# Another order of the first stage of an attention and SwiGLU kernel

## The chip, the cores and the metric

The kernel runs on one core of a Trainium2 chip. The metric is device time in microseconds (us) of one execution. The engines are TensorE (PE: matmuls; PEld is its weight load), VectorE (DVE), ScalarE (ACT), GpSimd (POOL) and SyncE (SP); each works through its own queue in order, and the engines wait for each other on semaphores. POOL, SP and ACT also issue DMA transfers.

## What is computed

Attention over 4 batches, 8 heads, 768 tokens and 64 channels, in which a query sees the 96 last keys and the 8 first (global) ones, with a bias that falls with distance; then a SwiGLU block on the 3072 tokens.

```
scores = scale * q @ k.T + bias        # bias = -slope[h] * dist, -1e9 outside the window
a      = softmax(scores)
x      = (a @ v) as 3072 x 512
g      = x @ w_gate                    # 512 x 1536
out    = (g * sigmoid(g) * (x @ w_val)) @ w_out
```

## The kernel before

The program is one string, ORDER, of steps such as `c.0.1.0`; a table, WORK, gives the function of each, and a loop calls them one after the other. So ORDER sets the order of the instructions in every engine's queue. An engine doesn't pass a waiting instruction. PSUM banks are handed out in the order of the string too: score and value products take turns on two double banks (`double`), all else takes the longest-freed of four single banks (`single`, `release`).

Work goes batch by batch. In a batch the heads are taken as four pairs (hp 0 to 3); keys are cut into seven chunks of 120, each with the 8 global keys in front; a batch's queries are two halves. For batch 0, a pair's scores are four units: u 0 and 1 for the first half, 2 and 3 for the second. Two groups g of two pairs make up the 512 channels of x. The block then runs on half batches t, with 12 column groups f of 128.

The steps that the text names, with their arguments and engine:

- `Lf`, `Lh.i.half.h0.h1`, `Lr.b.i.h`: rows of k (i = 0) or q (i = 1); `Lv.b.c`: rows of v of a chunk; `Lw.which.n.g`: gate (0) or value (1) weights of the columns 512 n on, upper or lower half of the rows; `LG`: global rows of v into vG; `L4`: rows of batch 1. All but Lf are issued by POOL.
- `fill.n` (L344): n warm products of 256 columns, whose results nobody reads.
- `cast` and `T.hp.half.i` (L363, TensorE transposes), `k.hp.half.e` (L371) and `q.hp.half.e` (L395), the copies out of PSUM by engine e; `U`, `kw`, `qw` are the same for pairs of batch 1; `D` is a transposing DMA and `K` spreads its keys.
- `sl.h` (L331, DVE): slope of a head times the identity; `B.hp.u` (L457, PE): writes the bias into a score bank; `c.b.hp.u` (L467, PE): adds the scores; `x.b.hp.u` (L481, ACT): the exponential.
- `M.h.part` (L336, ACT): mask of a head, 216 columns for part 0 and 432 for part 1; `m.b.hp.u.e` (L490): multiplies exponentials by the masks of the pair's two heads on engine e (P is POOL, V is VectorE). Units with a `B` need no mask.
- `G.b.c0.c1.e` (L274): copies the global rows of v from vG into the chunks c0 to c1 - 1 of vS, on e.
- `w.b.g.half.what` (L524, PE): denominators (what = 0, den) and values (1 and 2, num); `i`, `r` (DVE): inverts and spreads the denominators; `p.b.g.half.e` (L573): writes x.
- `g.t.f` and `v.t.f` (L582, PE): gate and value products, four matmuls each over the rows of the weights; `ga`, `gb` are the first and last two of a gate product; `t` (ACT, tanh), `s` and `h` (DVE); `o`, `e`: product with w_out and its copy to HBM.

The value products of batch 0's first half (`w.0.0.0.1`) read chunks 0 to 2 of vS; those of the second half (`w.0.0.1.1`) read chunks 2 to 6. `m.0.0.2.P` reads part 1 of the masks of heads 0 and 1, `m.0.3.1.P` that of heads 6 and 7.

Of the kernel before, what the change touches and what calls it, by code (L numbers as in the profile page):

```python
# [49 lines left out]
g.0.4 g.0.7 L4.1.0 t.0.4 h.0.0 s.0.4 t.0.7 s.0.7 g.0.6 t.0.6 L4.0.0 M.4.1 s.0.6 ga.0.2 gb.0.2 t.0.2  # L50
M.3.1 v.0.4 Lv.0.5 h.0.4 v.0.6 c.0.2.3 s.0.2 m.0.0.2.P c.0.2.2 x.0.2.3 h.0.6 x.0.2.2 w.0.0.1.0
i.0.0.1 r.0.0.1 g.0.5 t.0.5 G.0.4.7.P s.0.5 v.0.2 v.0.7 M.2.1 h.0.7 g.0.8 h.0.2 g.0.9 M.5.1 t.0.8
s.0.8 v.0.5 Lv.0.3 M.6.0 g.0.11 Lv.0.4 t.0.9 s.0.9 h.0.5 Lv.0.6 Lw.1.2.0 t.0.11 s.0.11 g.0.10 t.0.10
c.0.3.3 s.0.10 m.0.2.3.V m.0.2.2.P U.1.0 x.0.3.3 m.0.3.3.V U.0.1 U.1.1 kw.1.A U.0.0 qw.1.A w.0.0.1.1
w.0.0.1.2 p.0.0.1.V w.0.1.1.1 w.0.1.1.0 Lw.1.2.1 Lr.1.0.6 w.0.1.1.2 i.0.1.1 c.1.1.1 Lr.1.0.7 v.0.9
r.0.1.1 p.0.1.1.V kw.0.A Lr.1.1.7 qw.0.A v.0.8 x.1.1.1 h.0.8 h.0.9 M.7.0 v.0.10 Lr.1.0.4 g.1.6
Lr.1.1.4 c.1.0.0 t.1.6 x.1.0.0 c.1.0.1 D.1.3.0 v.0.11 h.0.11 h.0.10 g.1.0 t.1.0 s.1.0 x.1.0.1
c.1.1.0 g.1.9 t.1.9 g.1.7 s.1.6 t.1.7 s.1.9 g.1.1 s.1.7 x.1.1.0 g.1.3 v.1.0 t.1.3 Lr.1.0.5 h.1.0
v.1.6 D.1.2.0 c.1.0.2 s.1.3 h.1.6 c.1.1.2 K.1.3.A t.1.1 K.1.2.V g.1.5 s.1.1 x.1.1.2 M.2.0 M.0.0
v.1.9 h.1.9 v.1.7 t.1.5 h.1.7 Lr.1.1.6 Lr.1.1.5 D.1.3.1 s.1.5 g.1.2 t.1.2 x.1.0.2 s.1.2 D.1.2.1  # L60
v.1.5 g.1.11 t.1.11 h.1.5 m.1.0.1.P Lo.1 s.1.11 Lr.3.0.5 g.1.4 Lo.0 m.1.1.2.P v.1.3 h.1.3 t.1.4
m.1.0.2.V Lo.2 g.1.8 t.1.8 v.1.1 h.1.1 s.1.4 c.1.2.1 x.1.2.1 c.1.3.1 s.1.8 v.1.8 v.1.11 h.1.11 v.1.2
Lr.2.0.3 x.1.3.1 h.1.2 Lv.1.1 c.1.2.2 x.1.2.2 c.1.3.0 v.1.4 Lr.2.0.0 h.1.4 o.0.1.0 Z.1.V m.1.1.0.P
M.4.0 Lr.2.0.2 m.1.3.1.V G.1.0.7.S g.1.10 Lv.1.2 o.0.1.1 o.0.1.2 x.1.3.0 c.1.2.0 x.1.2.0 h.1.8
c.1.3.2 x.1.3.2 o.0.1.3 e.0.1 Lr.2.1.1 M.1.0 v.1.10 o.0.0.0 o.0.0.1 Lv.1.0 m.1.2.1.V m.1.1.1.V
Lr.2.0.1 t.1.10 m.1.3.0.V o.0.0.2 o.0.0.3 o.0.2.0 o.0.2.1 m.1.2.2.V Z.2.V Lv.1.3 s.1.10 m.1.0.0.V
w.1.0.1.0 e.0.0 w.1.0.0.1 w.1.0.0.0 h.1.10 m.1.2.0.P w.1.1.0.0 Lv.1.5 w.1.1.0.1 D.2.1.0 w.1.1.0.2
w.1.0.0.2 i.1.0.0 i.1.1.0 Lr.2.1.0 o.0.3.0 o.0.3.1 Lr.3.1.2 r.1.0.0 p.1.0.0.D D.2.0.0 o.0.3.2
o.0.3.3 Lv.1.6 r.1.1.0 Lv.1.4 Lr.2.1.4 p.1.1.0.D o.0.2.2 e.0.3 o.0.2.3 e.0.2 g.2.1 i.1.0.1 r.1.0.1
t.2.1 s.2.1 Lr.2.1.3 Lr.2.1.7 g.2.7 t.2.7 s.2.7 g.2.3 t.2.3 v.2.7 h.2.7 g.2.0 v.2.3 K.2.1.V Lr.3.0.1  # L70
g.2.5 s.2.3 K.2.0.V t.2.0 w.1.0.1.1 m.1.3.2.P w.1.1.1.1 w.1.1.1.0 D.2.0.1 s.2.0 w.1.1.1.2 Lr.2.1.2
D.2.1.1 i.1.1.1 w.1.0.1.2 o.0.4.0 t.2.5 s.2.5 Lr.2.0.7 Lr.2.0.6 o.0.4.1 o.0.4.2 o.0.4.3 p.1.0.1.D
v.2.0 h.2.3 e.0.4 Lr.3.1.4 h.2.0 n.1.1.1 g.2.4 t.2.4 r.1.1.1 p.1.1.1.P D.2.3.0 v.2.1 h.2.1 s.2.4
g.2.11 t.2.11 s.2.11 g.2.2 t.2.2 Lr.2.0.4 v.2.4 h.2.4 g.2.6 t.2.6 Lr.2.0.5 s.2.2 s.2.6 v.2.5 g.3.5
t.3.5 c.2.1.1 Lr.2.1.5 x.2.1.1 c.2.0.0 x.2.0.0 h.2.5 v.2.6 s.3.5 D.2.2.0 g.3.4 g.2.10 t.2.10
Lr.2.1.6 c.2.0.1 Lv.3.5 c.2.1.0 x.2.1.0 K.2.3.V h.2.6 v.2.11 s.2.10 h.2.11 Lr.3.0.3 v.2.2 o.0.5.0
g.3.3 x.2.0.1 h.2.2 t.3.4 g.2.8 t.2.8 Lr.3.0.0 m.2.0.0.V m.2.0.1.P o.0.5.1 o.0.5.2 s.2.8 s.3.4
o.0.5.3 D.2.3.1 e.0.5 Lr.3.1.6 v.2.10 h.2.10 v.3.5 t.3.3 g.3.10 t.3.10 D.3.0.0 c.2.0.2 h.3.5 s.3.10
g.3.6 t.3.6 Lr.3.1.3 g.2.9 x.2.0.2 s.3.3 v.2.8 h.2.8 t.2.9 v.3.10 D.2.2.1 G.2.0.7.S c.2.3.0 h.3.10
x.2.3.0 s.3.6 c.2.3.2 x.2.3.2 m.2.1.1.P K.2.2.A o.1.0.0 v.3.4 o.1.0.1 o.1.0.2 m.2.1.0.P v.2.9  # L80
m.2.3.2.V s.2.9 h.2.9 w.2.0.0.0 i.2.0.0 h.3.4 c.2.2.1 c.2.2.0 g.3.9 r.2.0.0 x.2.2.0 Lr.3.0.7 g.3.7
x.2.2.1 t.3.9 s.3.9 o.1.0.3 e.1.0 Lv.2.0 c.2.1.2 x.2.1.2 c.2.3.1 v.3.9 h.3.9 v.3.6 h.3.6 D.3.1.1
t.3.7 Lv.2.1 x.2.3.1 g.3.11 t.3.11 Lr.3.0.2 v.3.7 Lv.2.2 g.3.8 m.2.3.0.P t.3.8 m.2.2.0.P s.3.7 h.3.7
m.2.3.1.V v.3.3 h.3.3 s.3.8 w.2.0.0.1 w.2.0.0.2 m.2.2.1.P w.2.1.0.0 i.2.1.0 r.2.1.0 Lv.3.4 Lr.3.0.4
w.2.1.0.1 w.2.1.0.2 Lr.3.1.0 D.3.1.0 s.3.11 g.3.1 t.3.1 K.3.1.A g.3.2 t.3.2 s.3.1 s.3.2 o.1.1.0
o.1.1.1 p.2.1.0.D Lr.3.1.7 o.1.1.2 o.1.1.3 g.3.0 v.3.11 e.1.1 t.3.0 p.2.0.0.D s.3.0 v.3.1 g.4.9
Lv.2.3 c.3.1.0 x.3.1.0 t.4.9 h.3.11 h.3.1 c.3.1.1 v.3.2 h.3.2 v.3.8 h.3.8 g.4.5 Lr.3.1.1 x.3.1.1
t.4.5 s.4.5 g.4.6 t.4.6 Z.3.V D.3.0.1 Lv.2.4 c.3.1.2 x.3.1.2 c.2.2.2 x.2.2.2 s.4.6 v.4.9 v.4.5 s.4.9
h.4.9 h.4.5 v.3.0 h.3.0 g.4.8 K.3.0.A t.4.8 v.4.6 s.4.8 v.4.8 m.2.1.2.P Lv.2.6 o.1.2.0 o.1.2.1
m.2.2.2.V D.3.3.1 o.1.2.2 h.4.6 Lv.3.2 g.4.2 t.4.2 h.4.8 m.3.1.2.V D.3.2.0 c.3.0.0 x.3.0.0 w.2.1.1.0  # L90
Lv.2.5 K.3.2.A m.2.0.2.P w.2.0.1.0 i.2.0.1 i.2.1.1 w.2.1.1.1 w.2.1.1.2 w.2.0.1.1 w.2.0.1.2 r.2.1.1
o.1.5.0 r.2.0.1 Lr.3.1.5 D.3.2.1 g.4.11 o.1.5.1 o.1.5.2 Lv.3.6 o.1.2.3 p.2.1.1.D o.1.5.3 p.2.0.1.D
Lr.3.0.6 c.3.2.2 e.1.2 e.1.5 s.4.2 c.3.2.1 g.4.1 t.4.1 g.5.7 s.4.1 o.1.4.0 o.1.4.1 o.1.4.2 t.5.7
s.5.7 t.4.11 x.3.2.2 m.3.1.0.P s.4.11 v.5.7 o.1.4.3 h.5.7 v.4.2 e.1.4 g.5.6 h.4.2 t.5.6 g.4.0 v.4.1
x.3.2.1 o.1.3.0 m.3.2.1.P t.4.0 s.5.6 o.1.3.1 s.4.0 h.4.1 D.3.3.0 g.4.4 t.4.4 s.4.4 g.4.7 c.3.0.2
x.3.0.2 Lv.3.1 c.3.0.1 o.1.3.2 o.1.3.3 x.3.0.1 e.1.3 v.4.11 K.3.3.V c.3.2.0 c.3.3.2 h.4.11 x.3.3.2
m.3.3.2.P t.4.7 v.5.6 h.5.6 v.4.4 Lv.3.3 h.4.4 g.5.8 x.3.2.0 v.4.0 v.5.8 m.3.2.0.P s.4.7 t.5.8 s.5.8
# [591 lines left out]
```

## Time and profile before

| | |
|---|---|
| Time, median of 3 runs | 241.35 us (241.26 to 241.36) |
| Profiled execution | 241.18 us |
| Its span, first to last instruction | 239.4 us |
| TensorE busy | 232.8 us, 97% of the span |
| VectorE, ScalarE, POOL busy | 159.0, 117.5, 128.4 us |
| TensorE busy from 0 to 6 / 6 to 9 / 9 to 12 / 12 to 15 us | 4.80 / 2.93 / 2.24 / 2.29 |
| TensorE busy from 15 to 19 / 24 to 37 / 60 to 220 us | 4.00 / 13.00 / 159.75 |
| TensorE, warm products (26) | until 7.6 to 8.1 us in four groups |
| DMA read from HBM | 28.52 MB |

Times in the profile's rows are from the start of the span. A row of the timeline has start, length, engine, line, operation, output and input tiles and the number of instructions merged in it; in brackets stands how long its engine sat idle before it and what ended that. In the row of 40 slices, a digit is a tenth of busy time. In the chain of waits a row is start, length and what ran. A DMA row has the tensor, the issuing queue, the number of transfers, their size and the time from issue to landing.

### The profile page before, as it was taken

The numbers are of one execution on the slowest core, as the hardware profiler recorded it, in microseconds if no ns is written. First come the engines' busy times: TensorE is split into PE (matmuls) and PEld (weight loads), VectorE is DVE, ScalarE is ACT, GpSimd is POOL, SyncE is SP. The second block draws the span as 40 slices with busy tenths as digits, with TensorE's granted clock in tenths as the row PEclk, the third lists the DMA queues.
The fourth block names the chain that finished last, engine by engine and source line by source line (L and its number), as shares of the span: only waits on it lengthen the run. The fifth ranks groups of instructions, "written<-read, shape, count | busy, mean of one in ns | idle before, by whom it ended". The sixth has DMA issues, their size and how long they took to land.

```text
span 239.4 us, 5661 instructions
## 1 busy us (share of the span) xinstructions
PE 232.8 (97%) x2284; PEld 133.5 (56%) x2284; DVE 159.0 (66%) x351; ACT 117.5 (49%) x225; POOL 128.4 (54%) x136
## 2 busy tenths in 40 slices
PE   8889999999999999999999999999999999999994
PEld 5555666555455655546555555556566555565452
DVE  4697888787769676677876844687878843577000
ACT  3878777876405355666474446652142323232121
POOL 8996887599899098999974004799100000000000
PEclk9999999999999999999999999999999999999999
DMA  7999999999999999997999025413020110200042
GB/s 174 179 191 205 204 171 155 149 153 179 161 139 147 170 147 123 176 100 126 126 151 107 3 88 93 72 11 23 0 90 3 44 42 10 83 1 0 0 178 88
DMA packets 88714, 25.50 MB, mean 107 GB/s; under 512 B 78536, under 2 KB 85744, under 8 KB 88688
## 3 DMA queue, kind: packets, MB, share of 16 engines
q0 software_dynamic: 67520, 13.81, 69.9%
q1 hardware_dynamic: 20624, 10.94, 21.7%
q10 hardware_dynamic: 544, 0.39, 0.6%
q8 instruction: 18, 0.29, 0.5%
q14 instruction: 8, 0.07, 0.1%
HBM read 28.52 MB, written 6.29 MB: 145 GB/s over the span
## 4 chain that ended last, share of the span: by engine, by line
PE 94%; DVE 3%; ACT 2%; issue 0%; ACTq 0%
PE gps L588 27%; PE vps L588 26%; PE ops L623 25%; PE sc L475 5%; PE num L538 4%; PE den L538 2%; PE warm L346 2%; PE trs L367 1%; ACT at L485 1%; PE sc L462 1%; DVE at L503 1%; PE trs L405 1%; DVE slopeI L332 1%; DVE qT L396 0%; DVE xT L575 0%; ACT osb L633 0%
## 5 line engine op out<-in xcount | busy, mean ns | idle before, releaser
L588 PE MATMUL gps<-xT,wg 128*128 128x408 f16 (+1 forms) x384 | 72.9, 326 | 0.0
L595 ACT ACTIVATE th<-gps 128x360 f32<-128x360 f32 (+1 forms) x96 | 46.5, 492 | 52.9 <-PE gps L588 47.8
L588 PE MATMUL vps<-xT,wv 128*128 128x408 f16 (+1 forms) x384 | 72.5, 326 | 0.0
L610 DVE TENSOR_TENSOR hT<-vps,sl 128x360 f16<-128x360 f32 (+3 forms) x108 | 52.8, 509 | 23.6 <-PE vps L588 22.1
L600 DVE SCALAR_TENSOR_TENSOR sl<-th,gps 128x360 f32<-128x360 f32 (+1 forms) x96 | 51.5, 548 | 23.9 <-ACT th L595 22.5
L623 PE MATMUL ops<-wo,hT 128*128 128x512 f16 (+1 forms) x300 | 67.0, 371 | 0.0
L503 POOL TENSOR_TENSOR at<-at,masks 128x432 f16<-128x432 f16 (+3 forms) x36 | 47.8, 1347 | 28.9 <-ACT at L485 27.7
L588 PEld LDWEIGHTS <-wv 128*128 128x128 f16 x384 | 36.7, 98 | 26.8 <-issue 1.4
L588 PEld LDWEIGHTS <-wg 128*128 128x128 f16 x384 | 36.7, 98 | 25.6 <-issue 0.7
L485 ACT ACTIVATE at<-sc 128x864 f16<-128x864 f32 (+2 forms) x52 | 42.3, 841 | 13.0 <-PE sc L475 12.8
L623 PEld LDWEIGHTS <-hT 128*128 128x128 f16 x300 | 28.8, 98 | 30.0 <-issue 0.2
L633 ACT ACTIVATE osb<-ops 128x512 f32<-128x512 f32 (+1 forms) x25 | 14.3, 580 | 48.9 <-PE ops L623 45.5
L265 POOL DMA_DIRECT2D vS<-in_v_dram x28 | 25.6, 919 | 1.6 <-DVE vS L283 1.4
L306 POOL DMA_DIRECT2D qst<-in_q_dram x20 | 17.1, 869 | 0.0
L306 POOL DMA_DIRECT2D kst<-in_k_dram x20 | 17.1, 858 | 0.0
L575 DVE TENSOR_TENSOR xT<-num,rb 128x720 f16<-128x720 f32 (+1 forms) x15 | 14.1, 948 | 1.5 <-PE num L538 1.0
L475 PE MATMUL sc<-qT,kT 64*128 64x216 f16 (+4 forms) x232 | 14.7, 240 | 0.3
L475 PEld LDWEIGHTS <-kT 64*128 64x128 f16 x232 | 8.1, 94 | 9.6 <-issue 7.7
L555 DVE STREAM_TRANSPOSE dT<-den 128x384 f32<-128x384 f32 (+1 forms) x16 | 9.5, 595 | 4.7 <-PE den L538 4.4
L503 DVE TENSOR_TENSOR at<-at,masks 128x864 f16<-128x864 f16 (+2 forms) x21 | 10.5, 537 | 1.9 <-ACT at L485 1.9
L538 PE MATMUL num<-at,vS 128*32 128x216 f16 (+4 forms) x512 | 11.6, 233 | 0.0
L538 PEld LDWEIGHTS <-vS 128*32 128x32 f16 x512 | 9.1, 96 | 1.3 <-issue 1.1
(58 smaller groups left out, 117.1 us busy)
## 6 DMA issues: line engine op xcount, KB each, us to landing
out_dram<-osb SPq DMA_DIRECT2D x23, 256.0 KB, 2.1
vS<-in_v_dram POOLq DMA_DIRECT2D x24, 120.0 KB, 5.7
kst<-in_k_dram POOLq DMA_DIRECT2D x20, 96.0 KB, 5.2
qst<-in_q_dram POOLq DMA_DIRECT2D x20, 96.0 KB, 5.2
wg<-in_moe_w_gate_dram POOLq DMA_DIRECT2D x6, 256.0 KB, 8.5
wv<-in_moe_w_val_dram POOLq DMA_DIRECT2D x6, 256.0 KB, 7.9
wo<-in_moe_w_out_dram POOLq DMA_DIRECT2D x3, 512.0 KB, 8.4
k<-in_k_dram POOLq DMA_DIRECT2D x3, 192.0 KB, 5.9
```

Source lines behind the costliest of these rows:

```text
L265: nc.gpsimd.dma_start(out=v_of(b)[NG:NG + n, c, :, :], in_=v[b, :, KC * c:KC * c + n, :].rearrange("h p d -> p h d"))
L306: nc.gpsimd.dma_start(out=rows_of(i, b, h // 2)[:, :, h % 2, :], in_=KQ[i][b, h].rearrange("(t p) d -> p t d", p=128))
L475: nc.tensor.matmul(sc[:, hi, col:col + n], lhsT=kTs[hp][r, 128 * c:128 * c + 128], rhs=qTs[b, hp][r, q0:q0 + n], start=fresh, stop=True, s ...
L485: nc.scalar.activation(out=at[:, :, 0:w], in_=scs.pop((b, hp, u))[:, :, 0:w], func=AF.Exp, scale=scale)
L503: ENG[e].tensor_mul(a2, a2, m[:, :, m0:m0 + n])
L538: nc.tensor.matmul(dst[r, o:o + n], lhsT=vSs[b][:, c, 4 * g + j, what - 1::2] if what else ones[:, 0:32], rhs=ats[b, hp, u][:, j % 2, col: ...
L588: nc.tensor.matmul(gv[t, f, which][:, 0:n], lhsT=w[:, c, 128 * f:128 * f + 128], rhs=xTs[t][:, c, 0:n], start=(c == 0), stop=(c == NC - 1))
L595: nc.scalar.activation(out=th[:, 0:n], in_=gv[t, f, 0][:, 0:n], func=AF.Tanh, scale=0.5)
L600: nc.vector.scalar_tensor_tensor(out=sl[:, 0:n], in0=gv[t, f, "t"][:, 0:n], scalar=1.0, in1=gv[t, f, 0][:, 0:n], op0=AluOp.add, op1=AluOp. ...
L610: nc.vector.tensor_mul(hT[:, f, at:at + c1 - c0], gv[t, f, 1][:, c0:c1], gv[t, f, "s"][:, c0:c1])
L623: nc.tensor.matmul(ops_t[key][:, 0:c.stop - c.start], lhsT=hT[:, f, r0:r0 + 128], rhs=wo[:, f, c], start=(f == 0), stop=(f == NFF - 1))
L633: nc.scalar.mul(out=osb[:, 0:n], in_=ops_t[key][:, 0:n], mul=0.5)
```

## The change

Only the string ORDER changes; no function does. The steps are the same but for three `fill` products fewer and another cut of one copy. In order:

- `fill.14 ... fill.2` ahead of the first transposes becomes `fill.10`; `fill.4` comes behind `T.0.0.1 q.0.0.V`; `fill.7` becomes `fill.6`.
- `G.0.1.4.P` becomes `G.0.1.3.A`: ScalarE copies the global rows of chunks 1 and 2, ahead of the first exponentials. `G.0.4.7.P` becomes `G.0.3.7.P`: POOL copies chunk 3 with the later ones.
- `c.0.1.1 x.0.1.1` go ahead of `c.0.1.0 x.0.1.0`, each exponential directly behind its scores.
- `sl.5 q.2.0.V` go ahead of `T.3.0.1 q.3.0.V`.
- Masks later: `M.6.1 M.7.1` behind `x.0.3.1`; `M.1.1` behind `t.0.6`; `M.0.1` behind `t.0.2`; `M.5.0` behind `g.0.9`.

The lines of the diff that hold all of this (the rest of the diff is the same steps with other line breaks):

```diff
-LG Li Z.0.P pre fill.14 sl.2 fill.2 Lf.A.1.0 cast.1.0.V sl.6 Ld.S T.0.0.1 q.0.0.V sl.3 Lf.A.1.1 dd
-cast.1.1.A sl.1 T.1.0.1 fill.7 Lf.S.0.1 cast.0.1.V Lh.0.0.4.8 T.1.0.0 k.1.0.V sl.0 Lf.S.0.0
-cast.0.0.V B.1.1 B.1.0 fill.3 q.1.0.A c.0.1.0 M.5.0 c.0.1.1 M.1.1 T.0.0.0 k.0.0.V T.3.0.0 sl.4
-k.3.0.V M.0.1 x.0.1.0 x.0.1.1 Lh.1.0.4.8 T.2.0.0 M.6.1 k.2.0.A M.7.1 B.0.0 c.0.0.0 x.0.0.0 B.0.1
-c.0.0.1 x.0.0.1 T.2.0.1 T.3.0.1 q.3.0.V Lh.1.1.0.4 Lh.0.1.0.4 sl.5 T.1.1.0 Lh.1.1.4.8 q.2.0.V
-T.1.1.1 q.1.1.A Lv.0.1 k.1.1.V T.0.1.1 c.0.3.1 Lv.0.2 Lv.0.0 B.2.0 Lh.0.1.4.8 Lw.0.0.0 x.0.3.1
-c.0.2.0 q.0.1.V Lw.1.0.0 T.0.1.0 w.0.0.0.0 Lw.0.0.1 x.0.2.0 T.2.1.1 T.3.1.1 B.2.1 c.0.2.1 q.2.1.A
-sl.7 B.3.0 x.0.2.1 q.3.1.A G.0.1.4.P c.0.3.0 x.0.3.0 Lw.1.0.1 M.3.0 w.0.0.0.1 i.0.0.0 Lw.0.1.0
...
-g.0.4 g.0.7 L4.1.0 t.0.4 h.0.0 s.0.4 t.0.7 s.0.7 g.0.6 t.0.6 L4.0.0 M.4.1 s.0.6 ga.0.2 gb.0.2 t.0.2
-M.3.1 v.0.4 Lv.0.5 h.0.4 v.0.6 c.0.2.3 s.0.2 m.0.0.2.P c.0.2.2 x.0.2.3 h.0.6 x.0.2.2 w.0.0.1.0
-i.0.0.1 r.0.0.1 g.0.5 t.0.5 G.0.4.7.P s.0.5 v.0.2 v.0.7 M.2.1 h.0.7 g.0.8 h.0.2 g.0.9 M.5.1 t.0.8
...
+LG Li Z.0.P pre fill.10 sl.2 Lf.A.1.0 cast.1.0.V sl.6 Ld.S T.0.0.1 q.0.0.V fill.4 sl.3 Lf.A.1.1 dd
+cast.1.1.A sl.1 T.1.0.1 fill.6 Lf.S.0.1 cast.0.1.V Lh.0.0.4.8 T.1.0.0 k.1.0.V sl.0 Lf.S.0.0
+cast.0.0.V B.1.1 B.1.0 fill.3 q.1.0.A G.0.1.3.A c.0.1.1 x.0.1.1 c.0.1.0 x.0.1.0 T.0.0.0 k.0.0.V
+T.3.0.0 sl.4 k.3.0.V Lh.1.0.4.8 T.2.0.0 k.2.0.A B.0.0 c.0.0.0 x.0.0.0 B.0.1 c.0.0.1 x.0.0.1 T.2.0.1
+sl.5 q.2.0.V T.3.0.1 q.3.0.V Lh.1.1.0.4 Lh.0.1.0.4 T.1.1.0 Lh.1.1.4.8 T.1.1.1 q.1.1.A Lv.0.1 k.1.1.V
+T.0.1.1 c.0.3.1 Lv.0.2 Lv.0.0 B.2.0 Lh.0.1.4.8 Lw.0.0.0 x.0.3.1 M.6.1 M.7.1 c.0.2.0 q.0.1.V Lw.1.0.0
+T.0.1.0 w.0.0.0.0 Lw.0.0.1 x.0.2.0 T.2.1.1 T.3.1.1 B.2.1 c.0.2.1 q.2.1.A sl.7 B.3.0 x.0.2.1 q.3.1.A
+c.0.3.0 x.0.3.0 Lw.1.0.1 M.3.0 w.0.0.0.1 i.0.0.0 Lw.0.1.0 m.0.3.1.P r.0.0.0 w.0.0.0.2 p.0.0.0.V
...
+s.0.1 v.0.3 h.0.3 v.0.0 x.0.0.2 v.0.1 Lw.0.2.0 h.0.1 g.0.4 g.0.7 L4.1.0 t.0.4 h.0.0 s.0.4 t.0.7
+s.0.7 g.0.6 t.0.6 L4.0.0 M.1.1 M.4.1 s.0.6 ga.0.2 gb.0.2 t.0.2 M.0.1 M.3.1 v.0.4 Lv.0.5 h.0.4 v.0.6
+c.0.2.3 s.0.2 m.0.0.2.P c.0.2.2 x.0.2.3 h.0.6 x.0.2.2 w.0.0.1.0 i.0.0.1 r.0.0.1 g.0.5 t.0.5
+G.0.3.7.P s.0.5 v.0.2 v.0.7 M.2.1 h.0.7 g.0.8 h.0.2 g.0.9 M.5.0 M.5.1 t.0.8 s.0.8 v.0.5 Lv.0.3 M.6.0
```

Steps behind these that the prediction names keep their order: on POOL `Lv.0.3 Lv.0.4 Lv.0.6 Lw.1.2.0 m.0.2.2.P Lw.1.2.1` and then the rows `Lr` of batch 1; on TensorE `w.0.0.1.1 w.0.0.1.2 w.0.1.1.1 w.0.1.1.0 w.0.1.1.2 c.1.1.1 v.0.9`.

## The prediction

> **What bounds the kernel now.** I read the page's 40 slices first, then the chain of waits, then the timelines of the first 45 us engine by engine, then the DMA issues one at a time. TensorE is full from about 14 us to the end, so a change of the first stage is worth what it moves the full stretch, and only if nothing inside that stretch starts to wait.
>
> ```profile
> PE   8889999999999999999999999999999999999994
> DMA  7999999999999999997999025413020110200042
> ...
> 8.59 1.20 ACT at L485 x2
> 9.83 0.52 PE sc L462 x2
> ...
> 11.55 0.56 DVE qT L396
> 12.10 1.26 DVE slopeI L332
> 13.36 0.47 DVE qT L396
> 13.88 0.36 PE sc L475 x4
> ```
>
> The last lines are the chain: it leaves TensorE for two exponentials (8.59), then for a query copy, a slope and a second query copy on VectorE (11.55 to 13.83). These are the waits that the change touches. The DMA row says the transfers are full as well.
>
> ```profile
> 12.02 1.34 DVE L332 TENSOR_SCALAR slopeI<-ident 128x128 f16<-128x128 f16 x1
> ...
> 11.85 1.45 POOL L280 COPY vS<-vG 8x1536 f16<-8x1536 f16 x1
> 18.78 0.70 POOL L313 DMA_DIRECT2D wg<-in_moe_w_gate_dram  x1 [0.33 <-DMA wv<-in_moe_w_val_dram]
> 20.39 0.75 POOL L295 DMA_DIRECT2D qst<-in_q_dram  x1 [0.91 <-DMA wg<-in_moe_w_gate_dram]
> 24.59 1.53 POOL L503 TENSOR_TENSOR at<-at,masks 128x208 f16<-128x208 f16 x2 [1.03 <-ACT at L485]
> 27.49 2.52 POOL L265 DMA_DIRECT2D vS<-in_v_dram  x3
> 33.18 0.75 POOL L313 DMA_DIRECT2D wv<-in_moe_w_val_dram  x1
> ...
> wg<-in_moe_w_gate_dram POOLq DMA_DIRECT2D x1, 256.0 KB, 8.7
> wv<-in_moe_w_val_dram POOLq DMA_DIRECT2D x1, 256.0 KB, 5.0
> ...
> 38.32 2.00 PE L588 MATMUL vps<-xT,wv 128*128 128x360 f16 x12
> ```
>
> Slope 5 and the copy of the global rows end together (13.36 and 13.30). POOL's issues at 18.78 and 20.39 each waited for the landing of the transfer issued eight before. The first single-issue line is Lw.0.0.1, issued 11.15, landed 19.85; the second is Lw.1.2.1, issued 33.18, landed 38.18, with its first user (v.0.9) in the last line at 38.3. These two landings decide my sum.
>
> **The front, part by part.** Warm products: 26 become 23. Sixteen took 3.59 us, 0.22 each; ten end near 3.4. VectorE's cast of q ends at 3.71, so T.0.0.1 starts at 3.75 instead of 4.72. T.1.0.1 doesn't move: ScalarE's cast waits for its q rows until 4.64 and ends at 5.15. Six warm products instead of seven after it (1.18 / 7 = 0.17) bring the first keys forward by 0.15; their landing (1.61 + 4.2 = 5.8) and cast (0.35) are earlier than that.
>
> ScalarE: M.5.0, M.1.1 and M.0.1 (1.29 us from 6.15) leave, G.0.1.3.A comes. Nothing like it is in the trace. Nearest rows: ScalarE's 128x384 copy, 0.48, and 128x768 copy, 0.86, give 0.99 ns an element, so 1024 elements take 1.1; bounds 0.86 (the 768 copy) and 1.45 (POOL's copy of 1536). It waits for vG (1.36 + 5.1 = 6.5) and ends at 7.6, at most 8.0. ScalarE was free from 7.44 to 8.59, and the first exponential can't come before 8.25, so it costs nothing; without that cover it would delay x.0.1.1 by its own length.
>
> Exponentials as banks come: x.0.1.1 (0.4) now goes ahead of x.0.1.0, so B.0.0 waits for the short one only: 9.1 instead of 9.83. c.0.0.0 then waits for k.0.0.V (9.67). M.6.1 and M.7.1 no longer stand before x.0.0.0, which starts at about 10.05 instead of 10.99. Slope 5 finds no POOL copy beside it: 0.2 instead of 1.34, and with q.2.0.V ahead of T.3.0.1 both query copies are done at 11.75 instead of 13.83. The two masks now stand between x.0.3.1 (12.05) and x.0.2.0: 2 x 0.45 put x.0.2.0 at 13.25 to 14.15, before 14.28 to 15.17. x.0.3.0 follows at 15.2 to 16.1 (16.55 to 17.44), w.0.1.0.0 at 16.1 (17.48), ga.0.0 at 17.7 (19.07). **Front gain: 1.35 us.**
>
> **Where the gain is capped.** From 6 to 33 us the transfers run at about 200 GB/s with a backlog of 7 to 11 us from issue to landing. Taking G.0.1.4.P (1.45) off POOL issues five weights earlier, but a full queue doesn't land them earlier. g.0.3 needs Lw.0.0.1, landed 19.85, and ran at 20.74: slack 0.85. g.0.4 (24.87) needs Lw.0.1.1: 15.45 + 8.4 = 23.85, slack 1.0. So of 1.35 I keep **0.84** here.
>
> **What the moved masks do behind it.** m.0.0.2.P multiplies by the masks of heads 0 and 1, made by M.0.1 and M.1.1. Before, both were made by 7.44 and POOL's idle 1.03 ended with x.0.0.2 (24.59). Now ScalarE makes them after t.0.6 and after t.0.2. Starts in its queue lie 0.45 apart for such a mask (27.10 to 27.55) and 0.35 for a tanh (27.55 to 27.90). With 0.84 gained, g.0.6 ends at 25.9; t.0.6 starts there, M.1.1 at 26.24, M.4.1 at 26.69, t.0.2 at 27.14, M.0.1 at 27.49, ending (0.56) at 28.05. So m.0.0.2.P runs from 28.1 to 29.6 (1.53) instead of from 24.59 to 26.1. Two things are behind it.
>
> First, on TensorE, w.0.0.1.0 needs this product. It would be reached at 28.1 and ends after 29.6: about 29.85, where it ended at 29.40. **The 0.84 is gone and 0.45 is lost.**
>
> Second, behind it in POOL's queue stand G.0.3.7.P, Lv.0.3, Lv.0.4, Lv.0.6, Lw.1.2.0, m.0.2.2.P, Lw.1.2.1 and the rows of batch 1. G copies four chunks instead of three: 1.45 x 4 / 3 = 1.94 (1.45 if its cost were fixed): until 31.55. Three value issues 2.52: 34.05. Lw.1.2.0 0.72: 34.8. m.0.2.2.P 1.53: 36.3. Lw.1.2.1 is issued at 36.3 instead of 33.18, **3.1 later**. The backlog that hid POOL's pauses before is used up: the last transfer ahead (Lv.0.5, 22.61 + 11.0) lands at 33.6. Later, with empty queues, 48 KB of V landed 3.0 after issue and 120 KB 3.5 after (at 118 and 146.9), 0.5 for 72 KB, so 256 KB need some 4.4; bounds 3.5 (the 120 KB) and 5.0 (this transfer before). The V rows land by 36.4, where w.0.0.1.1 is reached at 36.6: in time. Lw.1.2.1 lands at 36.3 + 4.4 = 40.7. v.0.9's third product needs it and ran at 38.39 + 2 x 0.15 = 38.7. **TensorE stands about 2.0 us later than before**; the 0.45 and p.0.0.1.V are inside that wait.
>
> What else is late: rows of batch 1, by 3.1. Their first transposing DMA (40.05 + 4.7 = 44.75) feeds K.1.3.A at 46.57: slack 1.8, plus the 2.0 that everything has moved, so it covers. M.5.0 (0.27) before t.0.8 takes an idle 0.37 of ScalarE. POOL was idle 3.86 before 44.38, so its own lateness ends there. Nothing later gives the 2.0 back: TensorE is busy 159.75 of the 160 us from 60 to 220.
>
> m.0.2.2.P now falls beside m.0.2.3.V (35.37 before). A VectorE mask beside POOL masks took 1.55 at 102.79 where 0.60 is usual, so Lw.1.2.1 may be up to 0.95 later; I put 0.1 on the sum for it.
>
> **Sum:** span 239.4 + 2.0 + 0.1 = 241.5. The profiled run took 241.18, 1.78 outside the span; the median shown is 241.35, 0.17 above that run. **Median 243.45.** Bounds: transfer 3.5 instead of 4.4 and G at 1.45, 242.05; no front gain (+0.84), transfer 5.0 (+0.6) and contention (+0.85), 245.7.
>
> [...] Matmuls of 256 columns started 0.21 apart until about 6.3 and 0.11 apart from 6.4, with TensorE busy since 1.2 and the profile's granted clock at full all the time. The change opens a pause of 0.3 at 3.4. By the row, clocking up comes when it came.
> [...]
>
> **Rivals.** (1) *Faster:* the weights land earlier once POOL issues them earlier, or m.0.0.2.P isn't late. It decides if M.0.1 ends before about 26.6 (28.1 less 1.53) and Lw.1.2.1 lands by 37.8 (38.7 less 0.84 and a tenth). Place: the end of the first-stage wait on VectorE; price: the 0.84, up to 1.35 without the cap. For it: the chain's 1.26 us slope. Against: ScalarE's order, in which M.0.1 can't precede t.0.2. Time 241.35 - 0.84 = 240.5 (240.0). (2) *Only the wait of w.0.0.1.0:* the backlog hides POOL's delay, Lw.1.2.1 lands before 39.1. For it: Lv.0.5 lands only at 33.6. Against: 36.3 plus even 3.5. Time 241.35 + 0.45 = 241.8. (3) *The change doesn't do what it says:* slope 5 stays slow without the POOL copy (others took 0.43 to 0.52 beside DMA issues) and transposes ahead open new pauses. Front gain near 0, everything behind 0.84 later: 244.3.
>
> **Chances.** Forecast 0.64 (its own range 242.4 to 244.4), rival 1 0.15, rival 2 0.12, rival 3 0.09. The likeliest gives 243.4. The range leaves out rival 1 and a bit above: 241.6 to 244.8. A difference under 0.2% (0.48 us) can't be told from none here. Faster by more: rival 1, 0.15. Within: half of rival 2 and a little of the forecast's lower edge, 0.08. Slower: 0.77.
>
> **What would show it.** Right: slope 5 near 0.2; B.0.0 near 9.1; ga.0.0 near 17.7; TensorE pausing before g.0.3 at 19.9; m.0.0.2.P near 28 with ScalarE's masks as releaser; TensorE idle over 1 us before the den of w.0.0.1.0; Lw.1.2.1 issued near 36; a pause inside v.0.9 until near 40.7. Wrong: weights landing a microsecond earlier, TensorE without pause from 24 to 40, or warm products still 0.21 apart after 6.4.

## The result, and the profile after

| | before | changed kernel, first measurement | changed kernel, measured again (e5) |
|---|---|---|---|
| Median | 241.31 us (4 executions) | 246.88 us (4: 246.27 to 248.58) | 244.27 us (6: 243.65 to 245.48) |
| Ratio to before, 95% interval | | 1.0244 [1.0214, 1.0273] | 1.0118 [1.0092, 1.0145] |
| Span of the profiled execution | 239.4 us | 245.5 us | 242.2 us |

The change makes the kernel slower: by 5.6 us in the first measurement and by 2.9 us in the second, which had its own runs of the kernel before beside it (median 241.35). The forecast was 2.1 us. The two measurements differ by more than either's interval, so there are two things to explain: a loss of about 3 us that is there in both, and some 2.6 us by which the first measurement, with all four executions, lies above the second. In all that follows, medians are over every execution, and ratios leave out the few that took over 1.5% longer than the fastest of their kernel.

The page of the changed kernel, the rows of 40 slices (6.1 us each) for TensorE, the granted clock and the transfers:

```profile
PE   7999796999999999999999999999999999999994
PEclk9999999799999999999999999999999999999999
DMA  7999999959999999999999322533020101200043
GB/s 164 179 191 205 204 90 145 142 84 167 169 152 163 189 101 158 144 147 107 132 133 148 35 85 76 74 22 20 3 85 3 45 0 43 85 4 0 0 149 110
```

Counted from 0, TensorE is no longer full in slices 4 and 6 (24.5 to 30.7 and 36.8 to 43 us). The granted clock shows a 7 in slice 7, where every slice of before has a 9; and the transfers, at 204 GB/s in slice 4, drop to 90 in slice 5 (171 before). TensorE behind slice 7 is as before: from 60 to 220 us TensorE is busy 159.75 us in both kernels. So the loss lies ahead of 60 us. The chain of waits through it (start, length, what ran; rows left out are TensorE's own work):

```profile
27.18 1.01 ACT masks L337 x2
28.19 0.36 ACT th L594
28.55 0.46 ACT masks L337
29.01 0.08 issue
29.09 1.53 POOL at L502 x2
...
32.42 2.53 POOL vS L264 x3
34.94 0.71 POOL wv L312
35.66 1.49 POOL at L502 x2
37.15 5.97 DMA wv<-in_moe_w_val_dram
43.12 0.05 issue
43.17 2.61 PE vps L587 x10
```

Before, the chain stood on TensorE from 14 us to 100 us, but for 1.02 us of VectorE at 36.97. Now it leaves it at 27 us for the masks that the change made late, goes through POOL's whole queue (the product m.0.0.2.P at 29.09, the copy, three transfers of V rows, a weight, a second product) and ends in the transfer of Lw.1.2.1, 5.97 us long, on which v.0.9 waits. TensorE's timeline shows what that costs:

```profile
29.72 0.23 PE L537 MATMUL den<-at,ones 128*32 128x104 f16 x4 [0.67 <-POOL at L502]
30.68 0.46 PE L537 MATMUL den<-at,ones 128*32 128x216 f16 x16 [0.73 <-POOL at L502]
...
38.79 1.17 PE L537 MATMUL num<-at,vS 128*32 128x216 f16 x52 [0.65 <-DMA vS<-in_v_dram]
...
41.05 0.48 PE L587 MATMUL vps<-xT,wv 128*128 128x360 f16 x2
43.17 2.61 PE L587 MATMUL vps<-xT,wv 128*128 128x360 f16 x10 [1.63 <-DMA wv<-in_moe_w_val_dram]
45.58 1.57 PE L587 MATMUL gps<-xT,wg 128*128 128x408 f16 x4
```

Three waits: 1.40 us for the masked exponentials (den, w.0.0.1.0), 0.65 for V rows (num, w.0.0.1.1), 1.63 for the weight (inside v.0.9). And behind the last one the products run at half rate: ten in 2.61 us, and four of 408 columns in 1.57, where four took 0.85 later. The windows of the same execution give the clock for it (stretch, its length, busy time and instructions of each engine, granted clock, DMA share, GB/s):

```profile
43.20:45.60 2.40, 2.40 (x11) 1.29 (x12) 1.44 (x4) 0.00 (x0) 1.28 (x2) 0.62 2.13 135
45.60:47.20 1.60, 1.60 (x7) 0.56 (x7) 0.00 (x0) 0.02 (x1) 0.00 (x0) 0.50 2.53 159
47.20:50.00 2.80, 2.80 (x25) 1.42 (x23) 1.33 (x3) 2.17 (x4) 0.00 (x0) 1.00 0.73 126
```

TensorE is busy in all three, but with 0.62 and 0.50 of its clock until 47.2; in finer windows the 0.50 holds from about 43.8, some 3.4 us.

The front, where the gain was to come from, has this beginning on TensorE:

```profile
5.56 0.53 PE L366 MATMUL trs<-ident,q 128*64 128x128 f16 x6 [0.33 <-ACT q L349]
6.02 1.46 PE L345 MATMUL warm<-ones 128*128 128x256 f16 x6
7.41 0.53 PE L366 MATMUL trs<-ident,k 128*64 128x128 f16 x6
...
8.81 0.85 PE L345 MATMUL warm<-ones 128*128 128x256 f16 x3
```

Six warm products in 1.46 and three in 0.85 are 0.21 apart, still the half rate; it ended at about 9.6 us, where it had ended at 6.4 before. The granted clock doesn't show this one; it reads 1.00 for the stretch (the third figure from the end of the row):

```profile
6.00:10.00 4.00, 4.00 (x29) 2.08 (x29) 1.63 (x6) 1.64 (x3) 4.00 (x6) 1.00 1.57 184
```

The slope that had taken 1.34 us did take 0.18 (at 11.85), but ga.0.0 came at 19.16 against 19.07 before. There is no front gain in this execution.

### The profile page after: what moved, and what is told of

It reads as the page before. It is cut to its first block, busy times and chain, and to the rows that moved or that the text cites. A ratio compares the mean times of both kernels' runs of the same rounds, so it can differ in the third digit from the quotient of the medians.

```text
span 245.5 us, 5656 instructions
## 1 busy us (share of the span) xinstructions
PE 235.9 (96%) x2281; PEld 133.6 (54%) x2281; DVE 158.4 (65%) x351; ACT 118.4 (48%) x226; POOL 127.2 (52%) x135
## 4 chain that ended last, share of the span: by engine, by line
PE 87%; DMA 4%; POOL 3%; ACT 2%; DVE 1%; issue 1%; ACTq 0%
PE gps L587 25%; PE ops L622 25%; PE vps L587 24%; PE sc L474 5%; PE num L537 3%; DMA wv<-in_moe_w_val_dram 2%; PE den L537 2%; PE sc L461 2%; DMA q<-in_q_dram 2%; PE trs L366 1%; POOL at L502 1%; POOL vS L264 1%; PE warm L345 1%; ACT at L484 1%; DVE at L502 1%
## 5 line engine op out<-in xcount | busy, mean ns | idle before, releaser
L587 PE MATMUL vps<-xT,wv 128*128 128x408 f16 (+1 forms) x384 | 73.6, 329 | 1.6 <-DMA wv<-in_moe_w_val_dram 1.6
```

The lines of the kernel that those rows point to most:

```text
L587: nc.tensor.matmul(gv[t, f, which][:, 0:n], lhsT=w[:, c, 128 * f:128 * f + 128], rhs=xTs[t][:, c, 0:n], start=(c == 0), stop=(c == NC - 1))
```

## The experiments

The theory: the masks M.1.1 and M.0.1, moved late, delay POOL's product m.0.0.2.P, and with it the transfers queued behind it; the three waits and the half rate follow from that. Rivals: the rearranged warm products cost the time (late full rate); the longer copy G.0.3.7.P, the slow transfer itself, or the moment of issue of Lw.1.2.1 sets the loss; and the half rate is something else than a consequence of the pause. Each experiment is a change of the string ORDER (two also add a function), measured beside the kernel before.

| | base and edit | median us | ratio to before | profiled span |
|---|---|---|---|---|
| e1 | changed kernel, warm products as before | 244.28 | 1.013 [1.006, 1.020] | 242.6 |
| e2 | changed kernel, the three masks early | 241.32 | 1.000 [0.995, 1.004] | 239.1 |
| e3 | before, M.1.1 and M.0.1 late | 245.54 | 1.015 [1.008, 1.022] | 242.6 |
| e4 | changed kernel, loads ahead of m.0.0.2.P | 244.50 | 1.014 [1.007, 1.022] | 242.2 |
| e5 | changed kernel again | 244.27 | 1.012 [1.009, 1.015] | 242.2 |
| e6 | e1 and e2 together | 241.63 | 1.001 [0.998, 1.004] | 239.0 |
| e7 | changed kernel, v.0.9 with 14 products more | 245.56 | 1.017 [1.014, 1.019] | 244.4 |
| e8 | e6, copy G.0.3.7.P behind Lw.1.2.0 | 241.29 | 1.000 [0.997, 1.002] | 241.6 |
| e9 | changed kernel, Lw.1.2.1 ahead of m.0.2.2.P | 243.98 | 1.010 [1.007, 1.014] | 242.0 |
| e10 | changed kernel, three loads ahead of Lw.1.2.1 | 249.48 | 1.034 [1.029, 1.038] | 247.4 |
| e11 | e10, v.0.9 with 24 products more | 247.14 | 1.023 [1.019, 1.027] | 245.3 |
| e12 | before, 4 warm products instead of 26 | 241.96 to 249.93 | | 245.9 |

### Masks or warm products: e1, e2, e3 and e6

e1 gives the changed kernel the warm products of before:

```diff
-LG Li Z.0.P pre fill.10 sl.2 ... T.0.0.1 q.0.0.V fill.4 ... T.1.0.1 fill.6
+LG Li Z.0.P pre fill.14 sl.2 fill.2 ... T.0.0.1 q.0.0.V ... T.1.0.1 fill.7
```

> The changed order with its warm products put back as they were before (sixteen ahead of the first transposes, seven ahead of the first keys). Theory A (four terms: half-rate TensorE until 9.6 us eats the front gain, 0.9; POOL issues Lw.1.2.1 late, 2.1 plus 0.8 that comes from the lost front; that transfer takes 6.0 instead of 4.4; half rate again after the wait, 1.6): products 0.11 apart from about 6.4, ga.0.0 near 18.2 instead of 19.16, about 0.8 off the time: 246.0 where the changed kernel has 246.9. Rival B (the warm products are the whole cause): back to 241.3 or below. Rival C (the clock in the front costs nothing, since weights land at their own time): no difference, 246.9.

e2 gives the changed kernel the masks at their old times:

```diff
-G.0.1.3.A ... x.0.3.0 ... t.0.6 L4.0.0 M.1.1 M.4.1 ... t.0.2 M.0.1 M.3.1 ... M.5.0 M.5.1
+M.1.1 G.0.1.3.A M.0.1 ... x.0.3.0 M.5.0 ... t.0.6 L4.0.0 M.4.1 ... t.0.2 M.3.1 ... M.5.1
```

> The changed order with M.1.1, M.0.1 and M.5.0 made early again (M.1.1 and M.0.1 around the copy of the global rows on ScalarE, M.5.0 behind x.0.3.0). Theory A: m.0.0.2.P runs near 24.7, Lw.1.2.1 is issued near 33.3, no pause before v.0.9, no second half-rate stretch: 241.4, that is the time of before plus 0.1 for the front. Rival B (warm products): the whole loss stays, 246.9. Rival D (POOL's copy of four chunks or the copy on ScalarE costs by itself): between 242 and 244.

e3 does that part alone, in the kernel before:

```diff
-c.0.1.1 M.1.1 ... k.3.0.V M.0.1 ... L4.0.0 M.4.1 ... t.0.2 M.3.1
+c.0.1.1 ... k.3.0.V ... L4.0.0 M.1.1 M.4.1 ... t.0.2 M.0.1 M.3.1
```

> The kernel before with one edit: M.1.1 behind t.0.6 and M.0.1 behind t.0.2, as in the change; everything else as before. Theory A: the whole loss is reproduced but for the longer copy of four chunks (0.4): m.0.0.2.P near 29.0, Lw.1.2.1 issued near 36.7, v.0.9 pausing, half rate after it: 246.0 to 246.6. Rival B (warm products): 241.3. Rival E (the masks cost only the wait of w.0.0.1.0, 1.7): 243.0.

e6 makes both edits of e1 and e2.

> The changed order with the early masks of e2 and the warm products of e1. Theory A: nothing of the loss is left, and the front gain is capped by the landing of the weights and of the V rows, as in e2: 240.9 to 241.3. Rival C (the front gain reaches the end once the product is in time): 240.2.

With the masks early (e2) the loss is gone: 1.000. POOL's timeline of e2:

```profile
23.88 1.53 POOL L502 TENSOR_TENSOR at<-at,masks 128x208 f16<-128x208 f16 x2
25.37 1.88 POOL L279 COPY vS<-vG 8x2048 f16<-8x2048 f16 x1
27.20 2.54 POOL L264 DMA_DIRECT2D vS<-in_v_dram  x3
...
32.31 0.75 POOL L312 DMA_DIRECT2D wv<-in_moe_w_val_dram  x1
```

m.0.0.2.P runs at 23.88 without a wait, where it ran at 29.09, and Lw.1.2.1 is issued at 32.31 instead of 37.15. TensorE has no wait over 0.4 us behind the start. The reverse is e3: those two masks late in the kernel before, and nothing else changed, give a span 3.2 us longer, with the same waits in the same places on TensorE:

```profile
28.92 0.23 PE L537 MATMUL den<-at,ones 128*32 128x104 f16 x4 [0.67 <-POOL at L502]
29.88 0.46 PE L537 MATMUL den<-at,ones 128*32 128x216 f16 x16 [0.73 <-POOL at L502]
...
38.11 1.02 PE L537 MATMUL num<-at,vS 128*32 128x216 f16 x52 [0.78 <-DMA vS<-in_v_dram]
...
41.86 1.70 PE L587 MATMUL vps<-xT,wv 128*128 128x360 f16 x10 [1.15 <-DMA wv<-in_moe_w_val_dram]
```

So the two masks are the cause of the loss that both measurements share, shown from both sides: e2 removes it, and e3 makes it with nothing else. Warm products as before (e1) leave the loss: 1.013, with Lw.1.2.1 issued at 36.40, landed at 41.8, and a wait of 1.0 us in v.0.9. Against the first measurement of the changed kernel e1 looks like a gain of 2.6 us, but e5 below, with no edit, has the same median.

e2 and e6 also say what the rest of the change is worth. In e6 ga.0.0 came at 17.96, 1.1 before the profile of before, and the value products behind g.0.3 at 21.88 instead of 22.86; but v.0.9 came only 0.44 earlier (37.88 against 38.32) and the span is 0.4 shorter, within what executions differ by. What eats the rest is mostly w.0.0.1.1, which needs Lv.0.6, landed at 35.92 in e2: its first sixty products took 1.62 us there, and 1.16 in e4, where the rows had long been there. Behind it v.0.9 meets Lw.1.2.1, which landed at 38.3 in e2 and at 38.18 before, though e2 issued it 0.9 earlier. An earlier front moved neither landing.

### The same kernel again: e5

No edit.

> The changed kernel as it is, timed again beside the others of this set. Theory A: its executions differ by when TensorE reaches the full rate (products 0.21 or 0.11 apart) in the first 10 us and by whether it falls to half rate behind the pause before v.0.9: from 244.4 (neither) to 248 (both). Rival G (its level is fixed and the other kernels were measured on a luckier chip): all executions within 0.5 of 246.9.

In its profiled execution the front came nearly as forecast (ga.0.0 at 17.99 for 17.7) and no half rate followed the pause. Lw.1.2.1 on POOL, its transfer (the last figure is the time from issue to landing), and then what TensorE waited for until 60 us (engine, line, releaser: total, times, longest):

```profile
35.89 0.75 POOL L312 DMA_DIRECT2D wv<-in_moe_w_val_dram  x1
...
wv<-in_moe_w_val_dram POOLq DMA_DIRECT2D x1, 256.0 KB, 5.6
...
PE vps L587 <- DMA wv<-in_moe_w_val_dram: 1.5, 1, 1.5
PE den L537 <- POOL at L502: 1.4, 2, 0.7
...
PE num L537 <- DMA vS<-in_v_dram: 0.4, 1, 0.4
```

1.5, 1.4 and 0.4: the same three waits, 3.3 us, and a span 2.8 us longer. The profile of the first measurement is 3.3 us longer: 1.2 in the front (19.16 against 17.99; 0.3 of it because T.1.0.1 waited for its q rows), 0.4 by the transfer of Lw.1.2.1 (5.97 against 5.6) and some 1.6 of half rate. The mean clocks fit the last for three of the four executions of that measurement: 0.992, 0.993, 0.992 and 1.0, and 3.4 us at half clock take 0.007 off a mean over 245. In e5 one of six shows 0.993, and it is the longest of them (245.48). But the fourth, at 1.0, still took 246.27, 2.0 above e5's median, without a profile of its own. A late full rate in its front, which the clock doesn't show, would explain 1.2 of that; the rest is open. Rival G's fixed level is out, since e5's executions are 1.4 to 3.3 below it. A difference between chips isn't wholly out: e1 to e4, e5 to e8 and e9 to e12 ran on three chips, and for the first measurement none is on record. The kernel before had a median of 241.31 to 241.35 beside all four sets.

### The queue on POOL: e4, e8 and e9

e4 moves the five transfers ahead of the product that waits for the masks:

```diff
-m.0.0.2.P ... Lv.0.3 ... Lv.0.4 ... Lv.0.6 ... Lw.1.2.0 ... Lw.1.2.1
+Lv.0.3 Lv.0.4 Lv.0.6 Lw.1.2.0 Lw.1.2.1 m.0.0.2.P
```

> The changed order with the transfers Lv.0.3, Lv.0.4, Lv.0.6, Lw.1.2.0 and Lw.1.2.1 put ahead of m.0.0.2.P in POOL's queue; the masks stay late. It splits the two things behind the late product. Theory A: the transfers are issued between 24 and 30 us as earlier ones land, m.0.0.2.P still ends near 30.6, TensorE still waits 1.4 to 1.7 before the den of w.0.0.1.0, but v.0.9 doesn't pause and the clock stays full: 243.0. Rival E (the wait of w.0.0.1.0 is what costs, the transfers are hidden): 246.9 as the change. Rival F (TensorE's pauses alone, wherever they are, put the clock down): 244.5.

TensorE's timeline of e4:

```profile
30.75 0.23 PE L538 MATMUL den<-at,ones 128*32 128x104 f16 x4 [2.21 <-POOL at L503]
31.70 0.46 PE L538 MATMUL den<-at,ones 128*32 128x216 f16 x16 [0.72 <-POOL at L503]
...
41.08 2.00 PE L588 MATMUL vps<-xT,wv 128*128 128x360 f16 x12
```

The wait inside v.0.9 is gone: twelve products in 2.00, at 41.08. But the wait for m.0.0.2.P has grown from 1.40 to 2.93 us, because each of the five issues waited 0.3 to 0.7 us for an earlier landing and the product came at 30.11. The sum is what it was (244.50 against 244.27 in e5), and theory A's 243.0 was missed. The two waits are one delay: whatever stands first on POOL makes the other late. In this execution the clock stayed full behind the 2.93; two of the other three show mean clocks of 0.986 and 0.993, so half rate may have followed there.

e8 is e6 with the copy of the global rows behind Lw.1.2.0, so that the V rows are issued earlier (by 1.6 us against e6):

```diff
-G.0.3.7.P ... Lv.0.3 ... Lv.0.4 ... Lv.0.6 ... Lw.1.2.0
+Lv.0.3 ... Lv.0.4 ... Lv.0.6 ... Lw.1.2.0 G.0.3.7.P
```

> e6 with POOL's copy of the global rows of the chunks 3 to 6 put behind Lv.0.3, Lv.0.4, Lv.0.6 and Lw.1.2.0, which are then issued 1.9 earlier. In e2 the num of w.0.0.1.1 began with the landing of Lv.0.6 (35.92). Theory A: that landing moves to about 35, v.0.9 is limited by Lw.1.2.1 alone, and 0.4 to 0.8 of the front gain reaches the end: 240.6. Rival I (the queue is full, so an earlier issue lands no earlier): as e6, 241.1.

It equals before (1.000). TensorE's wait for the V rows in e6, then in e8:

```profile
35.70 1.08 PE L537 MATMUL num<-at,vS 128*32 128x216 f16 x52 [0.29 <-DMA vS<-in_v_dram]
```

```profile
36.11 1.09 PE L537 MATMUL num<-at,vS 128*32 128x216 f16 x52 [0.17 <-DMA vS<-in_v_dram]
```

Issued 1.6 earlier, the rows landed no earlier: theory A fails and rival I holds. In e2, whose masks are early too, 192 to 223 GB/s moved from 21 to 30.8 us. The longer copy is not a cost where the masks are early, and nothing here beat the kernel before. Its profiled span of 241.6 comes from another place: a transposing DMA landed late, and VectorE's copy at 91.49 us waited 2.79 for it (0.58 in the profile of before). The kernel before has spans of 241.6 to 242 in some executions too; whether by the same late landing, no trace shows.

e9 issues Lw.1.2.1 ahead of the second product:

```diff
-Lw.1.2.0 ... m.0.2.2.P Lw.1.2.1
+Lw.1.2.0 ... Lw.1.2.1 m.0.2.2.P
```

> The changed order with one step moved: Lw.1.2.1 ahead of m.0.2.2.P in POOL's queue instead of behind it, so it is issued 1.5 earlier and nothing but a product follows it for 1.5. Theory A (the issue of this one transfer sets the time, and its 5.4 to 6.0 us come from the rows of batch 1 that POOL issues right behind it): it takes 4.4, lands near 38.9, v.0.9 doesn't pause, and only the wait of w.0.0.1.0 and the short one of w.0.0.1.1 stay: 242.3, some 2 below the changed kernel (244.3 in the last set). Theory A2 (a lone transfer of this size takes 5.4 to 6.0 whatever follows): it lands near 40.2, a pause of 0.5 stays: 243.0. Rival E (the wait of w.0.0.1.0 is what costs): no difference, 244.3.

POOL's timeline, and then TensorE's, in e9:

```profile
34.24 1.42 POOL L312 DMA_DIRECT2D wv<-in_moe_w_val_dram  x2
35.68 1.54 POOL L502 TENSOR_TENSOR at<-at,masks 128x208 f16<-128x208 f16 x2
```

```profile
41.30 1.70 PE L587 MATMUL vps<-xT,wv 128*128 128x360 f16 x10 [0.63 <-DMA wv<-in_moe_w_val_dram]
```

Issued at 34.95, the weight took 6.3 us and landed at about 41.3. In e5, whose m.0.0.2.P ran 0.6 earlier, it was issued at 35.89 and landed at 41.5. Set against that product the issue came 1.5 earlier and the landing only 0.8. The median is 0.3 below e5's, so theory A (242.3) and A2 (243.0) both missed. One pair of profiles doesn't prove it, but an issue plus a fixed duration is not what they show. More likely the landing follows the five transfers that start within 5 us after the queue ran dry (two of 120 KB, one of 48 and two of 256): in the first profile the first took 3.5 us from issue to landing, and those behind it 5.3, 4.8, 5.4 and 6.0. This is argued and not shown: the rows of batch 1 are on their way as well before the weight lands, and Lw.1.2.1 took 6.0 to 6.1 in e2, e6 and e8 too, and in e2 no slice between 21 and 42 us was under 138 GB/s. The rates of the changed kernel between 21 and 44 us, in 40 slices of 0.58 us:

```profile
GB/s 207 228 191 201 198 212 201 207 201 205 207 209 198 205 199 200 203 193 163 113 31 14 4 65 153 60 85 105 136 191 156 73 146 177 153 163 128 143 149 135
```

About 200 GB/s until 31 us, then 31, 14 and 4 (32.5 to 34.2 us), and 60 to 190 while the five land. Before, no slice between 21 and 42 us was under 130.

### The half rate behind the pause: e7, e10, e11 and e12

e7 and e11 replace v.0.9 by a step that repeats the first of its four matmuls, for which the weights are there, so that TensorE works on while the rest lands; what is written at the end is unchanged.

```diff
-v.0.9
+vk.0.9.14
...
+    def kept_busy(t, f, times):
+        products(t, f, 1, 0, 0)
+        n = width_of(t % 2)
+        for i, c in enumerate([0] * times + list(range(NC))):
+            nc.tensor.matmul(
+                gv[t, f, 1][:, 0:n], lhsT=wv[:, c, 128 * f:128 * f + 128],
+                rhs=xTs[t][:, c, 0:n], start=(c == 0), stop=(i < times or c == NC - 1))
```

> The changed kernel, with the first product of v.0.9 repeated 14 times (2.1 us at the full rate) while its weights are on the way, so that TensorE isn't idle in that pause; the bank is started afresh by the real first product. Theory A: the wait stays, the half-rate stretch behind it goes: executions at 244.4 to 245.5, 1.5 below the changed kernel beside it where that shows the stretch. Rival H (the stretch has nothing to do with the pause): no difference from the changed kernel. If the wait is shorter than 2.1 us the repeats cost up to 0.5.

e7 alone decided nothing. It came out 1.3 us above e5, but its front had the late full rate (ga.0.0 at 19.20) and Lw.1.2.1 was issued at 37.18. Behind its repeats TensorE waited 0.44 and then ran at full rate; e5 had run at full rate behind 1.49 without any repeats. A longer pause was needed.

e10 makes the pause long by putting three more transfers ahead of Lw.1.2.1, and e11 adds the busy step to it:

```diff
-Lw.1.2.1 ... Lr.1.0.6 ... Lr.1.0.7 ... Lr.1.1.7
+Lr.1.0.6 Lr.1.0.7 Lr.1.1.7 Lw.1.2.1
...
-v.0.9
+vk.0.9.24
```

> The changed order with Lw.1.2.1 behind three of the rows of batch 1 (2.5 us of POOL's issuing), so that the pause before v.0.9 grows from 1.5 to about 4. Theory A: 2.5 more for the wait, and TensorE falls to half rate behind it in every execution (products 0.30 apart for some 3.4 us), 1.6 more: 248.4 where the changed kernel has 244.3. Rival H (the half rate behind the pause in the first trace had another cause): 246.8, products 0.15 apart behind the pause.

> e10 with the first product of v.0.9 repeated 24 times (3.7 us at the full rate) in that pause. Theory A: the wait stays and the half rate goes: 1.6 below e10, 246.8. Rival H: as e10. Repeats that outlast the wait would cost up to 0.5.

TensorE in e10, then in e11:

```profile
44.00 3.18 PE L587 MATMUL vps<-xT,wv 128*128 128x360 f16 x10 [4.41 <-DMA wv<-in_moe_w_val_dram]
46.98 1.57 PE L587 MATMUL gps<-xT,wg 128*128 128x408 f16 x4
```

```profile
39.25 4.14 PE L595 MATMUL vps<-xT,wv 128*128 128x360 f16 x26
44.13 0.48 PE L595 MATMUL vps<-xT,wv 128*128 128x360 f16 x2 [0.74 <-DMA wv<-in_moe_w_val_dram]
44.44 1.38 PE L587 MATMUL vps<-xT,wv 128*128 128x360 f16 x8
45.66 0.85 PE L587 MATMUL gps<-xT,wg 128*128 128x408 f16 x4
```

The weight is there at the same time in both (44.00 and 44.13). Behind 4.41 us of idleness ten products take 3.18 and four gate products 1.57; with TensorE kept busy the ten run from 44.13 to 45.82, 1.69, and the four take 0.85. The medians differ by 2.3 us, and every one of e10's six executions had a mean clock of 0.985 to 0.991, e11's 0.997 to 1.0. So the idle time in the pause causes the half rate here, and keeping TensorE busy with useless products avoids it. It is no remedy here, since the pause itself stays.

e12 takes nearly all warm products out of the kernel before:

```diff
-fill.14 ... fill.2 ... fill.7 ... fill.3
+fill.1 ... fill.1 ... fill.1 ... fill.1
```

> The kernel before with its 26 warm products cut to 4, everything else as before. It shows what a late onset of the full rate costs at the end. Theory A: products stay 0.21 apart (half rate) until 9.5 or later, ga.0.0 at 19.5 to 20.5 instead of 18.4 to 19.1, of which some 0.5 to 1.0 are hidden by the landing of the weights (19.9): 241.8 to 242.5. Rival C (the landing of the weights hides all of it): 241.35.

This run did not measure what it was made for. Its six executions lie between 241.96 and 249.93, too far apart for an interval. In the profiled one TensorE ran at half rate until about 9.9, and yet ga.0.0 came at 19.17 and v.0.9 only 0.1 later than before: up to there the late full rate cost 0.1 us in the order of before, where TensorE waited for slope 5 here too (0.27 us, 0.44 in the profile of before). The 6.5 us in its span arose elsewhere, at the transposing DMA that was late in e8's profile, for which VectorE waited 4.66 us this time. TensorE there:

```profile
91.60 0.78 PE L588 MATMUL vps<-xT,wv 128*128 128x360 f16 x4
95.31 1.36 PE L588 MATMUL vps<-xT,wv 128*128 128x360 f16 x4 [2.92 <-DVE hT L610]
```

Four products in 0.78 ahead of the wait of 2.92 and in 1.36 behind it: the half rate behind a pause once more, in another place (granted clock 0.50 from 95.3 to 98). Whether few warm products make that transfer late is open.

## Why the prediction was wrong in size

**Right: the place and the mechanism.** "What the moved masks do behind it" named ScalarE's order, the product m.0.0.2.P "from 28.1 to 29.6", and its two consequences. e2 and e3 confirm it. In e5 it ran from 27.83, w.0.0.1.0 ended at 29.81 (forecast 29.85), and POOL's copy took 1.88 (1.94). The forecast that Lw.1.2.1 is issued "at 36.3 instead of 33.18" stands against 35.89 in e5 and 37.15 in the first profile.

**Wrong: the transfer of Lw.1.2.1.** "So 256 KB need some 4.4; bounds 3.5 … and 5.0" is the step that failed in every profile with this order of the queue or one close to it: 6.0, 5.6, 5.4, 5.9, 6.3, 5.9, 5.5 and 5.2 in the first profile, e5, e1, e3, e9, e7, e10 and e11, all above the upper bound. I took the durations of two V transfers that POOL issued with no other right ahead of them. The trace of before had rows against it: of the three V transfers that POOL issued in a row from 118.37, the first, of 48 KB, took the 3.0 that I used, but the two of 120 KB behind it took 6.3 and 6.9. Here five start within 5 us of each other; that the landing follows the group is likely and not shown. In the same way "The V rows land by 36.4 … in time" failed: Lv.0.6, of 48 KB like the one at 118.37, took 4.8 (4.5 in e5) instead of 3.0, and TensorE waited 0.65 for the rows (0.41 in e5).

In e5 this is nearly all: landing at 41.5 against 40.7 forecast is 0.8, and its median, 244.27, is 0.8 above mine. The 0.1 for contention rests on a misread row: beside VectorE's mask at 102.79 POOL issued transfers (102.85 and 103.70) and ran no mask. In the first profile m.0.2.3.V came at the end of m.0.2.2.P, at 37.12, and took 1.12, as before.

**Wrong in the first measurement: the front gain.** "Front gain: 1.35 us" and "I keep 0.84" became −0.09 there and 1.08 in e5 (ga.0.0 at 19.16 and 17.99, 19.07 before). The single steps came as worked out (slope 0.18, ScalarE's copy of the global rows 1.04 for an estimate of 1.1, hidden), but the half rate lasted until 9.6, and B.0.0 came at 10.58 instead of 9.1. "By the row, clocking up comes when it came" failed: in the first profile, where the pause of 0.22 at 3.5 us is the one foretold, full rate came 3.2 us later than before; in e5, with a pause of 0.31, at about 7. Two executions of one kernel differ by 2.6 us in it, and no run shows what sets the moment. Between e5 and e7 (ga.0.0 at 17.99 and 19.20), which share the first stage and had no wait for q rows, the difference in the front is 1.2; in the first profile 0.3 of the 1.2 is that wait. The six transposes of the first keys tell it in one number: 0.36 us at full rate, 0.53 at half. All five profiles with 26 warm products (before, e1, e3, e6, e8) have 0.36; of eight with the change's 23, three have 0.53 (the first, e7, e9), and e11 has 0.38. That the rearranged products make the late moment more frequent is likely by these counts and not shown.

The cap was right, but only in small part for the reason given. TensorE waited 0.25 us in e1 and 0.20 in e8 for the weights of g.0.3, and not at all in e2 and e5. In e2 and e6 0.9 to 1.0 us of front gain lasted to 28 us; half of it was lost at w.0.0.1.1, which waits for the V rows.

**Missing: the half rate behind the pause.** No term of the sum had it; the sum took the pause at its length. It made some 1.6 us of the first profile and 2.3 us between e10 and e11.

The first profile adds up: 2.0 forecast; Lw.1.2.1 landed at 43.1 instead of 40.7, 2.4 (0.85 by its issue, from the front that gained nothing; 1.6 by the longer transfer); half rate 1.6. Together 6.0, and the span grew by 6.1.

**The rivals.** The faster case needed M.0.1 done by 26.6; it ended at 29.0 (27.8 even in e5's early front). "Only the wait of w.0.0.1.0" failed at its own condition, the landing of Lw.1.2.1 before 39.1. The third, a front gain near 0, happened in the first profile, though not by a slow slope: that was 0.18, as the change intended.

## What to carry to other kernels

Before a step is moved later, ask what stands behind its consumer in that engine's queue: here two masks of 0.45 us on an engine with time to spare held up POOL's product, and with it the issue of five transfers. A backlog hides an issuing engine's pauses only while it lasts (in the first profile POOL paused 5.37 us, and the rate fell from about 200 to 4 GB/s); once the queue has run dry, don't price the next landings by the duration of a lone transfer: here the first took 3.5 us, as a lone one had before (3.5), and Lw.1.2.1 behind it 6.0. V rows issued 1.6 us earlier into a full queue landed no earlier (e8). And a pause of TensorE can cost more than its length, since half rate may follow it (2.3 us between e10 and e11).

## What was unexpected of the hardware

- Half rate came in the middle of the kernel: behind 4.41 us of idleness (e10, in all six executions by their clocks), 2.92 (e12) and 1.63 (first profile, with 0.65 and 0.15 shortly before it), each with a granted clock of 0.50; but not, in the profiled executions, behind 2.21 and 0.72 (e4) nor 1.49 (e5). So the length of the last wait alone doesn't tell: 1.63, with others just ahead of it, was followed by half rate, and 2.21 was not.
- The granted clock reads 1.00 in the first 10 us of the first profile, while warm products there start 0.21 apart; in the middle of the kernel it reads 0.50 for the same rate.
- VectorE's slope beside POOL's copy of the global rows is slow in some executions only. In the profile of before the slope, started 0.17 behind the copy, took 1.34 us and the copy 1.45; in e3 the slope, started at 12.11, took 0.18, and the copy, started at 12.10, 1.51. The wait that the change set out to remove thus need not be in every execution of the kernel before, whose front differs from e3's by two masks on ScalarE. In e3 the two starts lie 0.01 apart; whether that decides it, no run shows.
